# Neighbourhood attention on one core: one two-bank P V tile and one normalization for both jobs of a pair, and a reordered first step

## The chip, the cores and the metric

The kernel runs on one core of a Trainium2 chip. Times are device microseconds (us). TensorE is called PE here (PEld is its weight load), VectorE DVE, ScalarE ACT, GpSimd POOL, SyncE SP. A profile shows one execution; a time given for a kernel is the median of its runs.

## The reference

The input is an image of 224 by 224 pixels with 192 channels. Every pixel attends to 49 neighbours: 7 rows by 7 columns with a distance of 2 between them, the window being moved inwards at the border.

```python
qkv = x @ wqkv                                  # C = 192
q, k, v = qkv[..., :C], qkv[..., C:2*C], qkv[..., 2*C:]
r0 = clip(ir - 6, 0, H - 1 - 12)                # 7 rows, 2 apart
c0 = clip(ic - 6, 0, W - 1 - 12)                # 7 columns, 2 apart
logits = einsum('bnc,bnkc->bnk', q, kn) * C ** -0.5
p = softmax(logits)
out = einsum('bnk,bnkc->bnc', p, vn) @ wo
```

## The kernel before

**Tiling.** As neighbours are 2 apart, the image falls into even and odd rows (`rc`) and even and odd columns (`cc`). A step is 16 rows of one row class: 14 steps, `steps` in line 573, row classes taking turns. A step has 14 slots `s` of 8 columns in each column class; a slot is a job, and jobs 2m and 2m+1 are pair m of the step. So there are 7 pairs in a step and 98 in all, numbered k.

**Operands.** The weights are multiplied together at the start (`AW` from Wq and Wk, `WP` from Wv and Wo). x is loaded transposed in 14 bands of 16 rows (`load_items`, line 145: three transposing DMAs on SP, of which the one with k = 1 fills `X1`, tile names xa and x). From a band, POOL copies (DVE for the first ones) make `XB` (`xb_items`, line 158) and the sorted strips `XS` (`sort_items`, line 167). Out of these PE makes, for a coming step, G (`g_items`, line 405: `whole` and `halves`, the latter through a tile gx that two POOL copies spread, line 460) and V (`v_item`, line 347: 8 matmuls into one bank, copied to `VF`). `VD` is V shifted by half a slot; it is filled by DMAs `vd_low` and `vd_high` (lines 354 and 358), in step 0 for the next step also by `first_vd`.

**A pair.** `stage1` makes the scores of both jobs in two PSUM banks and their maxima (nmx, DVE, line 503); `stage1b` the exponentials p (ACT, line 511). `stage2` transposes p on PE into one bank and copies it to pt_sb (DVE, line 523; ACT in most of the last step). `stage3` is P V: 16 matmuls for a pair, 8 for each job, into a bank o_ps for each job; columns 192 and 193 of it hold the sums of p. `stage4a` takes their reciprocals (rs, line 538), `stage4` multiplies (line 552; for the last three pairs the second job on ACT, line 550) into an SBUF tile o_sb and issues the output DMAs.

**Outputs.** A slot other than 0 is written by one DMA of 16 rows on SP (line 558), or, in the first and the last step where the 16 rows fall into two runs, by two, some of them on POOL. Slot 0 holds the border columns of both sides: 10 small DMAs (15 in the first and in the last step) go into a list `pool_q` and are issued by POOL (line 571), at most four entries of the list in a pass; copies for coming steps are put ahead of them. The slot's tile (o_s0) is read until the last of them has landed. Its pool has two buffers, that of the other slots (o_sb) six.

**Order.** The loop (line 629) is written out by hand and every engine keeps the order in which its instructions were issued (`in_order`). Pass k issues: scores of pair k; p of its first job; P V of pair k-2 and the normalization of its first job; G halves (`w64`); p of the second job; the transposes of pair k-1 and their copy; the normalization of the second job of pair k-2; then DMAs, one of the three loads of a coming band (`ld.pop`, line 679: passes 0, 1 and 2 of a step), and the G and V of the next step (`w128`). In step 0 the first two passes carry the 14 V items of step 0 itself as well.

**PSUM.** Eight banks: two for the scores, one for transposed p, two of pool `ps_o` for o_ps, three of pool `ps_g` that G, V and others take in turn. A buffer of a pool goes to the next tile when one is free, not in a fixed turn: the V tiles of the built program stand in banks 6, 5, 7, 6, 5, 7, 6, 7, 6, 6, 5, 7 and so on.

Of the kernel before, what the change touches and what calls it, by code (L numbers as in the profile page):

```python
# [21 lines left out]
NSLOT = 14  # L22
# [6 lines left out]
C = 192  # L29
# [37 lines left out]
def _win(t, p0, pn, off, dims):  # L67
    a = t[:]
    ps = a.ap[0][0]
    return bass.AP(a.tensor, a.offset + p0 * ps + off, [[ps, pn]] + [list(d) for d in dims])  # L70
# [28 lines left out]
def kernel(  # L99
# [15 lines left out]
    pers = ctx.enter_context(tc.tile_pool(name="pers", bufs=1))  # L115
    ps_s = ctx.enter_context(tc.tile_pool(name="ps_s", bufs=1, space=PSUM))
    ps_t = ctx.enter_context(tc.tile_pool(name="ps_t", bufs=1, space=PSUM))
    ps_o = ctx.enter_context(tc.tile_pool(name="ps_o", bufs=2, space=PSUM))
    ps_g = ctx.enter_context(tc.tile_pool(name="ps_g", bufs=3, space=PSUM))
    x1_p = ctx.enter_context(tc.tile_pool(name="x1", bufs=2))  # L120

# [182 lines left out]
            nc.gpsimd.memset(_win(t, 0, 128, 112 * rc, [[128, 8], [1, 16]]), 0.0)  # L304
    wT_lo = setup.tile([128, 3, C], BF, name="wT_lo")
    wT_hi = setup.tile([64, 3, C], BF, name="wT_hi")
    n_t = 0
    for X in range(3):
        for (dt_, d0, dn) in ((wT_lo, 0, 128), (wT_hi, 128, 64)):
            tp = (ps_o, ps_g)[n_t % 2].tile([128, 1024], BF, name="tp_w", tag=("o", "pg")[n_t % 2])  # L310
            n_t += 1
            nc.tensor.transpose(tp[0:dn, 0:128], w_lo[:, X * C + d0: X * C + d0 + dn], ident[:])
            nc.tensor.transpose(tp[0:dn, 128:192], w_hi[:, X * C + d0: X * C + d0 + dn], ident[0:64, 0:64])
            nc.scalar.copy(out=dt_[:, X, :], in_=tp[0:dn, 0:192])
# [25 lines left out]
    def v_mms(pv, at):  # L340
        for cc in range(2):
            for pas in range(2):
                for h in range(2):
                    k = 1 if pas else 2 * cc
                    nc.tensor.matmul(pv[64 * h:64 * h + 64, cc * C:(cc + 1) * C], lhsT=at(k, h), rhs=WP[(cc, pas)][:], start=(pas == 0), stop=(pas == 1))  # L345

    def v_item(rc, cb):
        def emit(dve):
            pv = ps_g.tile([128, 512], F32, name="pv", tag="pg")
            v_mms(pv, lambda k, h: XS[rc][:, k, cb, 64 * h:64 * h + 64])  # L350
            evac(_win(VF[rc], 0, 128, cb * VP, [[193, 2], [1, C]]), pv[:, 0:2 * C].rearrange("p (t c) -> p t c", c=C), dve)
        return emit
# [52 lines left out]
    def g_items(rc, ti, s0, ns):  # L405
        rows = row_runs(rc, ti)
        w = 8 * ns

        def mm(pg, cc, p0, c0):

            out_ = []
            for (d0, dn, mem, pair) in col_runs(cc, 8 * s0, 8 * s0 + w):
                for (j, n, par, r) in rows:
                    o = _win(pg, p0, 64, j * w + d0, [[w, n], [1, dn]])
                    for pas in range(2):
                        X = (XA, XB)[pas][mem]
                        out_.append((o, AW[(mem, pas)][:, c0:c0 + 64], _win(X, 0, 128, _x(par, r, pair), [[RW, n], [1, dn]]), pas))
            return out_

        def both(a, b):  # L420
            for q in range(max(len(a), len(b))):
                for l_ in (a, b):
                    if q < len(l_):
                        (o, l, r, pas) = l_[q]
                        nc.tensor.matmul(o, lhsT=l, rhs=r, start=(pas == 0), stop=(pas == 1))  # L425

        def put(dst, off, pg, dve, p0=0, pn=128):

# [12 lines left out]
        def whole(cc):  # L441
            def emit(dve):
                pg = ps_g.tile([128, 512], F32, name="pg", tag="pg")
                both(mm(pg, cc, 0, OUT_A[cc]), mm(pg, cc, 64, OUT_A[cc] + 64))
                put(G[rc][cc], s0 * 128, pg, dve)
            return emit

        def halves(dve, direct=False):
            pg = ps_g.tile([128, 512], F32, name="pgh", tag="pg")
            pg1 = ps_o.tile([128, 512], F32, name="pgh", tag="o") if direct else pg  # L450
            both(mm(pg, 0, XDAT[0], OUT_B[0]), mm(pg1, 1, XDAT[1], OUT_B[1]))
            if direct:
                put(G[rc][0], (NSLOT + s0) * 128, pg, False, XDAT[0], 64)
                put(G[rc][1], (NSLOT + s0) * 128, pg1, True, XDAT[1], 64)
                return
            gx = work.tile([128, 512], BF, name="gx", tag="gx", bufs=3)
            put(gx, 0, pg, dve)
            for cc in range(2):
                p = XDAT[cc]
                nc.gpsimd.tensor_copy(out=G[rc][cc][p:p + 64, 1, s0:s0 + ns, :], in_=gx[p:p + 64, 0:ns * 128].rearrange("p (s q) -> p s q", q=128))  # L460

        return [whole(0), whole(1), halves]
# [59 lines left out]
        J.pt = work.tile([128, 8, 128], BF, name="pt_sb", tag="pt_sb")  # L522
        (nc.scalar.copy if J.n == NSTEP - 1 and J.m < 5 else nc.vector.tensor_copy)(out=J.pt[:], in_=pt_ps[:])  # L523

    def stage3(J, ab):
        rc, s = J.rc, 2 * J.m + ab
        o_ps = (ps_o if J.k < NP - 1 else ps_g).tile([128, 512], F32, name="o_ps", tag="o" if J.k < NP - 1 else "pg")
        V = (VD[rc], VF[rc])
        for cc in range(2):
            for q in range(2):  # L530
                for h in range(2):
                    nc.tensor.matmul(o_ps[64 * h:64 * h + 64, cc * 193:cc * 193 + 193], lhsT=J.pt[:, 4 * ab + 2 * cc + q, 64 * h:64 * h + 64],  # L532
                                     rhs=V[h][:, (s - 1 + q) % NSLOT, cc * C:cc * C + 193], start=(q == 0), stop=(q == 1))
        J.o_ps[ab] = o_ps

    def stage4a(J, ab):
        J.rs[ab] = stat.tile([128, 2], F32, name="rs", tag="rs")
        nc.vector.reciprocal(out=J.rs[ab][:], in_=J.o_ps[ab][:, C:C + 2])
        return J.rs[ab]

    def stage4(J, ab):
        rc, ti, s, o_ps = J.rc, J.ti, 2 * J.m + ab, J.o_ps[ab]
        rs = J.rs.get(ab) or stage4a(J, ab)
        if s > 0:
            o_sb = work.tile([128, 2, C], BF, name="o_sb", tag="o_sb", bufs=6)
        else:
            o_sb = work.tile([128, 2, C], BF, name="o_s0", tag="o_s0")
        if J.k >= NP - 3 and ab == 1:
            for cc in range(2):
                nc.scalar.mul(o_sb[:, cc, :], o_ps[:, 194 * cc:194 * cc + C], rs[:, cc:cc + 1])  # L550
        else:
            nc.vector.tensor_tensor(out=o_sb[:], in0=_win(o_ps, 0, 128, 0, [[194, 2], [1, C]]),  # L552
                                    in1=rs[:].unsqueeze(2).to_broadcast([128, 2, C]), op=ALU.mult)
        prow = _rows(rc, ti)
        if s > 0:
            for (j0, nj, r0, rstep) in _aff_runs(prow):
# [18 lines left out]
    for n, (ti, rc) in enumerate(steps):  # L575
        for m in range(7):
            J = Pair()
            J.n, J.ti, J.rc, J.m, J.k, J.o_ps, J.s, J.rs = n, ti, rc, m, len(pairs), {}, {}, {}
            pairs.append(J)
    NP = len(pairs)  # L580

# [47 lines left out]
    for k in range(NP + 2):  # L629
# [20 lines left out]
        if k == NP:  # L650
            stage2(pairs[k - 1])
        if k >= 2:
            stage3(pairs[k - 2], 0)
            stage3(pairs[k - 2], 1)
            if k >= NP:
                stage4a(pairs[k - 2], 0)
                stage4a(pairs[k - 2], 1)
            stage4(pairs[k - 2], 0)
            if k == NP - 1:
                stage4a(pairs[k - 2], 1)  # L660
        for it in w64:
            it(False)
        if J:
# [1 line left out]
        if 1 <= k < NP:  # L665
            stage2(pairs[k - 1])
        if k >= 2:
            stage4(pairs[k - 2], 1)
        if not J:
            continue  # L670

        if m == 1 and 0 < n and n + 1 < NSTEP:
            vd_low(rc1, 9 if n == 1 else 7, 14)
        if n == 0 and m in (4, 6):
            vd_low(0, *((0, 5) if m == 4 else (5, 9)), nc.scalar)
        if 0 < n and m == 5 and n + 2 < NSTEP:
            vd_low(J.rc, 0, 7)
        if ld:
            ld.pop(0)()
        for i, it in enumerate(w128):  # L680
            it(n == 0 and i % (2 if m < 3 else 3) == 1)
            if n == 0 and it is v0[6]:
                vd_high(0, 13, 14)
                vd_high(0, 0, 6)
            if n == 0 and it is v0[13]:
                vd_high(0, 6, 13)
            if it is vs[6]:
                vd_high(rc1, 0, 7)
            if it is vs[13]:
                vd_high(rc1, 7, 14)  # L690
# [67 lines left out]
```

## Time and profile before

| | us |
|---|---|
| median of 3 runs (lowest, highest) | 364.18 (363.53, 366.75) |
| the profiled execution | 362.85 |
| its span, first to last instruction | 361.1 |
| PE busy in the span | 335.6 |
| DVE, ACT, POOL busy | 313.7, 307.5, 285.6 |
| first pair's scores start | 19.6 |
| first slot of steps 0, 1, 2, 3 normalized | 36.5, 67.1, 91.7, 114.3 |

In the profile an engine is busy while an instruction runs on it; a wait is put down to the instruction that ended last before it. A group has its line, engine, operation, the tiles written and read, and a count. The matmuls' ends are modelled. The last row of the table tells where the steps lie: later ones follow every 21.8 to 23.5 us, step 0 takes 30.5 and step 1 24.6 us.

### The profile page before, as it was taken

How to read it: one execution, taken by the hardware profiler on the slowest of the kernel's cores; microseconds unless marked ns; L12 is line 12 of the kernel's file. 1: busy time of each engine (PE TensorE's matmuls, PEld its weight loads, DVE VectorE, ACT ScalarE, POOL GpSimd, SP SyncE). 2: the span in 40 equal slices, each digit the busy share in tenths (PEclk: the TensorE clock that was granted, in tenths of full speed). 3: DMA queues.
4: the chain of work that ended last, by engine and by line, in shares of the span. 5: the costliest groups of instructions: out<-in, count | busy, mean ns of one | idle time of the engine just before them, and what ended most of it. 6: DMA issues, size and time to landing. Idle time of an engine off the chain costs nothing.

```text
span 361.1 us, 19455 instructions
## 1 busy us (share of the span) xinstructions
PE 335.6 (93%) x8104; PEld 305.8 (85%) x8104; DVE 313.7 (87%) x743; ACT 307.5 (85%) x821; POOL 285.6 (79%) x456
## 2 busy tenths in 40 slices
PE   3988888998999999999999999999999999999881
PEld 1676777997999899999989999899999999999671
DVE  8967987887998998989989999898998889989992
ACT  3654767997998999989999999999989989999792
POOL 8976799999896986959969699696995878374094
PEclk9999999999999999999999999999999999999998
DMA  9999986697988979899799998988989965634432
GB/s 188 204 175 180 174 172 148 146 199 162 202 177 201 196 164 190 186 194 192 168 183 181 197 190 177 161 213 180 198 178 192 191 146 121 143 97 108 103 80 77
DMA packets 137778, 60.79 MB, mean 168 GB/s; under 512 B 88841, under 2 KB 137166, under 8 KB 137691
## 3 DMA queue, kind: packets, MB, share of 16 engines
q1 hardware_dynamic: 130133, 56.37, 78.3%
q0 software_dynamic: 5520, 1.73, 2.7%
q10 hardware_dynamic: 2038, 1.47, 2.2%
q8 instruction: 63, 1.03, 1.2%
q14 instruction: 24, 0.20, 0.2%
HBM read 0.29 MB, written 19.27 MB: 54 GB/s over the span
## 4 chain that ended last, share of the span: by engine, by line
PE 69%; POOL 10%; DVE 8%; ACT 6%; DMA 3%; issue 2%; SPq 1%; POOLq 0%; DVEq 0%; ACTq 0%
PE pv L345 16%; PE s L501 15%; PE o_ps L532 14%; PE pg L425 10%; PE pt_ps L521 9%; PE pgh L425 5%; POOL out_dram L571 4%; ACT p L511 3%; DVE xb L160 2%; POOL xs L170 2%; POOL out_dram L558 2%; DMA out_dram<-o_sb 1%; DMA vd<-vf 1%; ACT vf L335 1%; DVE nmx L503 1%
## 5 line engine op out<-in xcount | busy, mean ns | idle before, releaser
L511 ACT ACTIVATE p<-s,nmx 128x224 bf16<-128x224 f32 x392 | 149.8, 450 | 24.5 <-DVE nmx L503 22.8
L503 DVE TENSOR_REDUCE nmx<-s 128x2 f32<-128x392 f32 (+1 forms) x196 | 102.4, 564 | 19.9 <-PE s L501 19.4
L552 DVE TENSOR_TENSOR o_sb<-o_ps,rs 128x384 bf16<-128x384 f32 x179 | 99.8, 557 | 7.1 <-DMA out_dram<-o_sb 0.9
L460 POOL COPY g<-gx 64x512 bf16<-64x512 bf16 (+1 forms) x110 | 61.8, 562 | 52.9 <-ACT gx L335 47.1
L345 PE MATMUL pv<-wp,xs 128*64 128x192 bf16 x1624 | 92.7, 250 | 7.1 <-POOL xs L170 1.9
L345 PEld LDWEIGHTS <-xs 128*64 128x64 bf16 x1624 | 78.5, 111 | 20.5 <-issue 8.8
L335 ACT CAST vf<-pv 128x384 bf16<-128x384 f32 x193 | 87.6, 518 | 9.6 <-PE pv L345 5.2
L571 POOL DMA_DIRECT2D out_dram<-o_s x150 | 84.2, 568 | 1.1 <-issue 1.1
L532 PE MATMUL o_ps<-vd,pt_sb 128*64 128x193 bf16 x784 | 82.2, 246 | 2.9 <-ACT pt_sb L523 2.1
L501 PE MATMUL s<-xa,g 128*64 128x196 bf16 (+7 forms) x990 | 82.2, 233 | 1.6 <-issue 0.5
L532 PE MATMUL o_ps<-vf,pt_sb 128*64 128x193 bf16 x784 | 82.1, 246 | 0.0
L501 PE MATMUL s<-xb,g 128*64 128x196 bf16 (+7 forms) x990 | 81.8, 232 | 0.3 <-ACT g L335 0.3
L501 PEld LDWEIGHTS <-g 128*64 128x64 bf16 x1980 | 77.6, 110 | 3.6 <-issue 2.5
L532 PEld LDWEIGHTS <-pt_sb 128*64 128x64 bf16 x1568 | 71.3, 109 | 4.9 <-ACT pt_sb L523 3.2
L523 DVE COPY pt_sb<-pt_ps 128x1024 bf16<-128x1024 bf16 x93 | 63.7, 686 | 5.4 <-PE pt_ps L521 0.6
L521 PE MATMUL pt_ps<-ident,p 128*64 128x128 bf16 x1568 | 63.9, 219 | 0.0
L521 PEld LDWEIGHTS <-p 128*64 128x64 bf16 x1568 | 57.0, 110 | 5.2
L335 ACT CAST g<-pg 128x512 bf16<-128x512 f32 (+4 forms) x136 | 57.6, 471 | 2.0 <-PE pg L425 2.0
L425 PEld LDWEIGHTS <-aw 128*64 128x64 bf16 x1320 | 54.1, 110 | 4.1 <-issue 0.7
L425 PE MATMUL pg<-xb,aw 128*64 128x512 bf16 (+9 forms) x440 | 53.9, 269 | 0.6 <-DVE xb L160 0.6
L425 PE MATMUL pg<-xa,aw 128*64 128x512 bf16 (+9 forms) x440 | 52.0, 270 | 0.0
L170 POOL COPY xs<-xa 128x896 bf16<-128x896 bf16 x50 | 45.1, 928 | 1.4
(75 smaller groups left out, 282.8 us busy)
## 6 DMA issues: line engine op xcount, KB each, us to landing
vd<-vf SPq DMA_DIRECT2D x49, 336.9 KB
out_dram<-o_sb SPq DMA_DIRECT2D x156, 96.0 KB
out_dram<-o_sb SPq DMA_DIRECT2D x26, 78.0 KB
out_dram<-o_s POOLq DMA_DIRECT2D x78, 9.0 KB, 3.9
vd<-vf SPq DMA_DIRECT2D x2, 337.8 KB
vd<-vf ACTq DMA_DIRECT2D x2, 336.9 KB
xa<-in_x_dram SPq DMA_TRANSPOSE x28
out_dram<-o_s POOLq DMA_DIRECT2D x26, 15.0 KB, 3.1
```

The costliest lines, as they stand in the source:

```text
L335: nc.scalar.copy(out=out_, in_=in_)
L345: nc.tensor.matmul(pv[64 * h:64 * h + 64, cc * C:(cc + 1) * C], lhsT=at(k, h), rhs=WP[(cc, pas)][:], start=(pas == 0), stop=(pas == 1))
L425: nc.tensor.matmul(o, lhsT=l, rhs=r, start=(pas == 0), stop=(pas == 1))
L460: nc.gpsimd.tensor_copy(out=G[rc][cc][p:p + 64, 1, s0:s0 + ns, :], in_=gx[p:p + 64, 0:ns * 128].rearrange("p (s q) -> p s q", q=128))
L501: nc.tensor.matmul(o, lhsT=w, rhs=r, start=(pas == 0), stop=(pas == 1))
L503: nc.vector.tensor_reduce(out=nmx[:], in_=_win(s_ps, 0, 128, lo, [[256, 2], [16, 14], [1, 16 - lo]]), axis=AX.XY, op=ALU.max, negate=True)
L511: nc.scalar.activation(out=J.p[:, ab, cc, :, z:z + 112].rearrange("p q (r k) -> p q r k", k=8), in_=_win(s_ps, 0, 128, cc * 256, [[8, 2], ...
L521: nc.tensor.transpose(pt_ps[64 * h:64 * h + 64, 4 * ab + 2 * cc + q, :], J.p[:, ab, cc, q, 64 * h:64 * h + 64], ident[:])
L523: (nc.scalar.copy if J.n == NSTEP - 1 and J.m < 5 else nc.vector.tensor_copy)(out=J.pt[:], in_=pt_ps[:])
L532: nc.tensor.matmul(o_ps[64 * h:64 * h + 64, cc * 193:cc * 193 + 193], lhsT=J.pt[:, 4 * ab + 2 * cc + q, 64 * h:64 * h + 64], rhs=V[h][:, ( ...
L552: nc.vector.tensor_tensor(out=o_sb[:], in0=_win(o_ps, 0, 128, 0, [[194, 2], [1, C]]), in1=rs[:].unsqueeze(2).to_broadcast([128, 2, C]), op ...
L571: pool_q.append(lambda dst=dst, p=p, m=n * nj, cc=cc: nc.gpsimd.dma_start(out=dst.rearrange("j i c -> i j c"), in_=o_sb[p:p + m, cc, :]))
```

## The change

Both jobs of a pair get one tile of two banks (`ps_o` has now one buffer of that size), written by all 16 P V matmuls, then read by one reciprocal of 4 sums and one multiplication of 768 elements a partition into one o_sb tile for both jobs. Both stand ahead of the copy of transposed p; before, the second job's two stood behind it. The last three pairs keep the normalization in two parts. The o_sb tiles are now four of pair size; slot 0 has no tile of its own any more. Around the first step: the transposes of the weights use `ps_g` alone; in passes 0 and 1 the fourth and fifth V item take the two banks of `ps_o`; the two `vd_low` of step 0 are issued by SP instead of ACT; and the loads of step 0 are issued in passes 0, 2 and 4 instead of 0, 1 and 2.

```diff
-    ps_o = ctx.enter_context(tc.tile_pool(name="ps_o", bufs=2, space=PSUM))
+    ps_o = ctx.enter_context(tc.tile_pool(name="ps_o", bufs=1, space=PSUM))
...
-            tp = (ps_o, ps_g)[n_t % 2].tile([128, 1024], BF, name="tp_w", tag=("o", "pg")[n_t % 2])
-            n_t += 1
+            tp = ps_g.tile([128, 1024], BF, name="tp_w", tag="pg")
...
+    spare = []
+
     def v_item(rc, cb):
         def emit(dve):
-            pv = ps_g.tile([128, 512], F32, name="pv", tag="pg")
+            pv = spare.pop(0) if spare else ps_g.tile([128, 512], F32, name="pv", tag="pg")
...
-            pg1 = ps_o.tile([128, 512], F32, name="pgh", tag="o") if direct else pg
+            pg1 = ps_o.tile([128, 2, 512], F32, name="pgh", tag="o")[:, 0, :] if direct else pg
...
+    def stage3(J):
+        rc = J.rc
+        if J.k < NP - 1:
+            o = ps_o.tile([128, 2, 512], F32, name="o_ps", tag="o")
+            J.o_ps = [o[:, ab, :] for ab in range(2)]
+            J.o_2 = o
+        else:
+            J.o_ps = [ps_g.tile([128, 512], F32, name="o_ps", tag="pg") for ab in range(2)]
...
+    def stage4a(J, ab):
+        if J.rs is None:
+            J.rs = stat.tile([128, 2, 2], F32, name="rs", tag="rs")
+            J.o_sb = work.tile([128, 2, 2, C], BF, name="o_sb", tag="o_sb", bufs=4)
+        if ab is None:
+            nc.vector.reciprocal(out=J.rs[:], in_=_win(J.o_2, 0, 128, C, [[512, 2], [1, 2]]))
+        else:
+            nc.vector.reciprocal(out=J.rs[:, ab, :], in_=J.o_ps[ab][:, C:C + 2])
+
+    def stage4b(J, ab, eng):
+        if ab is None:
+            nc.vector.tensor_tensor(out=J.o_sb[:], in0=_win(J.o_2, 0, 128, 0, [[512, 2], [194, 2], [1, C]]),
+                                    in1=J.rs[:].unsqueeze(3).to_broadcast([128, 2, 2, C]), op=ALU.mult)
...
-            stage3(pairs[k - 2], 0)
-            stage3(pairs[k - 2], 1)
...
+            P = pairs[k - 2]
+            stage3(P)
+            if k < NP - 1:
+                stage4a(P, None)
+                stage4b(P, None, nc.vector)
+            else:
...
+            stage5(P, 0)
...
-            stage4(pairs[k - 2], 1)
+            if k >= NP - 1:
+                stage4b(P, 1, nc.scalar)
+            stage5(P, 1)
...
-            vd_low(0, *((0, 5) if m == 4 else (5, 9)), nc.scalar)
+            vd_low(0, *((0, 5) if m == 4 else (5, 9)))
...
-        if ld:
+        if ld and (n > 0 or m in (0, 2, 4)):
             ld.pop(0)()
+        if k < 2:
+            o = ps_o.tile([128, 2, 512], F32, name="pv", tag="o")
         for i, it in enumerate(w128):
+            if k < 2 and i in (3, 4):
+                spare.append(o[:, i - 3, :])
```

`stage5` holds the output DMAs as `stage4` had them.

More of the change, by code (lines that the diff above doesn't have):

```diff
@@ L306 @@
     wT_hi = setup.tile([64, 3, C], BF, name="wT_hi")
-    n_t = 0
     for X in range(3):
         for (dt_, d0, dn) in ((wT_lo, 0, 128), (wT_hi, 128, 64)):
-            tp = (ps_o, ps_g)[n_t % 2].tile([128, 1024], BF, name="tp_w", tag=("o", "pg")[n_t % 2])
-            n_t += 1
+            tp = ps_g.tile([128, 1024], BF, name="tp_w", tag="pg")
             nc.tensor.transpose(tp[0:dn, 0:128], w_lo[:, X * C + d0: X * C + d0 + dn], ident[:])
@@ L523, in stage2 @@
         (nc.scalar.copy if J.n == NSTEP - 1 and J.m < 5 else nc.vector.tensor_copy)(out=J.pt[:], in_=pt_ps[:])
-    def stage3(J, ab):
-        rc, s = J.rc, 2 * J.m + ab
-        o_ps = (ps_o if J.k < NP - 1 else ps_g).tile([128, 512], F32, name="o_ps", tag="o" if J.k < NP - 1 else "pg")
-        V = (VD[rc], VF[rc])
[L529 to L534, printed above, removed]
@@ L536, in stage4a @@
-    def stage4a(J, ab):
[L537 to L545, printed above, removed]
-        else:
-            o_sb = work.tile([128, 2, C], BF, name="o_s0", tag="o_s0")
-        if J.k >= NP - 3 and ab == 1:
+    def stage3(J):
[6 more added lines that the diff above has]
+            J.o_ps = [ps_g.tile([128, 512], F32, name="o_ps", tag="pg") for ab in range(2)]
+        V = (VD[rc], VF[rc])
+        for ab in range(2):
+            s = 2 * J.m + ab
+            for cc in range(2):
+                for q in range(2):
+                    for h in range(2):
+                        nc.tensor.matmul(J.o_ps[ab][64 * h:64 * h + 64, cc * 193:cc * 193 + 193], lhsT=J.pt[:, 4 * ab + 2 * cc + q, 64 * h:64 * h + 64],
+                                         rhs=V[h][:, (s - 1 + q) % NSLOT, cc * C:cc * C + 193], start=(q == 0), stop=(q == 1))
@@ new lines, in stage4a @@
+    def stage4a(J, ab):
+        if J.rs is None:
[3 more added lines that the diff above has]
+            nc.vector.reciprocal(out=J.rs[:], in_=_win(J.o_2, 0, 128, C, [[512, 2], [1, 2]]))
+        else:
+            nc.vector.reciprocal(out=J.rs[:, ab, :], in_=J.o_ps[ab][:, C:C + 2])
[3 more added lines that the diff above has]
+                                    in1=J.rs[:].unsqueeze(3).to_broadcast([128, 2, 2, C]), op=ALU.mult)
+        elif eng is nc.vector:
+            nc.vector.tensor_tensor(out=J.o_sb[:, ab], in0=_win(J.o_ps[ab], 0, 128, 0, [[194, 2], [1, C]]),
+                                    in1=J.rs[:, ab, :].unsqueeze(2).to_broadcast([128, 2, C]), op=ALU.mult)
+        else:
@@ L549, in stage4, with stage5 @@
             for cc in range(2):
[L550 to L553, printed above, removed]
+                nc.scalar.mul(J.o_sb[:, ab, cc, :], J.o_ps[ab][:, 194 * cc:194 * cc + C], J.rs[:, ab, cc:cc + 1])
+    def stage5(J, ab):
+        rc, ti, s, o_sb = J.rc, J.ti, 2 * J.m + ab, J.o_sb[:, ab]
@@ L577 @@
             J = Pair()
-            J.n, J.ti, J.rc, J.m, J.k, J.o_ps, J.s, J.rs = n, ti, rc, m, len(pairs), {}, {}, {}
+            J.n, J.ti, J.rc, J.m, J.k, J.s, J.rs = n, ti, rc, m, len(pairs), {}, None
             pairs.append(J)
@@ L652 @@
         if k >= 2:
-            stage3(pairs[k - 2], 0)
-            stage3(pairs[k - 2], 1)
[L655 to L660, printed above, removed]
+            P = pairs[k - 2]
[4 more added lines that the diff above has]
+            else:
+                stage4a(P, 0)
+                if k >= NP:
+                    stage4a(P, 1)
+                stage4b(P, 0, nc.vector)
+                if k == NP - 1:
+                    stage4a(P, 1)
+            stage5(P, 0)
         for it in w64:
```

## The prediction

> **What bounds the kernel now.** First the busy time by stage (us; PE, PEld, DVE, ACT, POOL, each with its count; clock, DMA share, GB/s).
>
> ```profile
> 17.00:50.00 33.00, 28.05 (x668) 23.72 (x666) 25.82 (x57) 20.42 (x57) 25.20 (x43) 1.00 1.11 183
> 50.00:64.00 14.00, 12.30 (x288) 10.50 (x286) 11.22 (x27) 10.38 (x29) 13.38 (x19) 1.00 0.68 152
> 64.00:97.00 33.00, 31.47 (x705) 28.26 (x703) 27.84 (x68) 29.14 (x79) 31.00 (x48) 1.00 0.83 171
> 97.00:325.00 228.00, 227.00 (x5766) 213.28 (x5763) 206.04 (x492) 213.16 (x577) 182.81 (x274) 1.00 0.88 177
> ```
>
> From 97 to 325 PE is busy for 227.0 of 228 us: an engine that gets lighter there gives back 1 us at the most. Idle PE lies in steps 0 and 1 (5.0 + 1.7 + 1.5 = 8.2 us from 17 to 97) and in the tail. Who ends those waits (us in total, times, longest), PE from 17 to 97:
>
> ```profile
> PE pv L345 <- POOL xs L170: 1.9, 3, 0.7
> PE pv L345 <- DVE g L333: 1.6, 2, 0.8
> PE pv L345 <- ACT g L335: 1.4, 4, 0.6
> ...
> PE o_ps L532 <- DMA vd<-vf: 0.5, 1, 0.5
> ```
>
> V waits for a bank to be copied out (DVE, ACT) or for its sorted strips (POOL). The POOL waits are the last ones, at 60.3 and 84 to 85.7 us, so the third view is POOL's instructions in order of time (start and duration in us):
>
> ```profile
> 52.59 0.58 POOL L558 DMA_DIRECT2D out_dram<-o_sb  x1
> 53.21 3.39 POOL L160 COPY xb<-x 64x1792 bf16<-64x1792 bf16 x2
> 56.66 1.80 POOL L170 COPY xs<-xa 128x896 bf16<-128x896 bf16 x2
> ```
>
> and the fourth the chain that ended last:
>
> ```profile
> 82.97 2.69 POOL xs L170 x3
> 85.66 0.04 issue
> 85.71 0.68 PE pv L345 x11
> ```
>
> POOL works from 43.14 to 85.65 without a pause over 0.13 us, and the V matmul of step 2 starts 0.06 us later. **So the end follows POOL's position in step 0, then PE.** When POOL copies band 3 (53.21) is the number to predict.
>
> **1. One normalization.** Per pair before: two reciprocals at 159 ns and two multiplications at 557, 1.43 us. The merged multiplication has no row; it costs no less than 557 (one of today's) and no more than 1114 (two). DVE's casts from f32 PSUM give a slope: 384 elements 560 ns, 512 elements 684, 0.97 ns an element, so 557 + 384 x 0.97 = 930; I take 0.95 us. With 0.16 for the reciprocal, 1.11: DVE gains 0.32 us a pair, 31 us in 95, behind a busy PE: nothing. [...]
>
> What moves is pt_sb, now behind the whole multiplication. A pass without G halves, DVE and then the weight load that reads pt_sb:
>
> ```profile
> 163.75 0.16 DVE L538 RECIPROCAL rs<-o_ps 128x2 f32<-128x2 f32 x1
> 163.94 0.56 DVE L552 TENSOR_TENSOR o_sb<-o_ps,rs 128x384 bf16<-128x384 f32 x1
> 164.42 0.68 DVE L523 COPY pt_sb<-pt_ps 128x1024 bf16<-128x1024 bf16 x1
> ```
>
> ```profile
> 165.63 0.11 PEld L532 LDWEIGHTS <-pt_sb 128*64 128x64 bf16 x1
> ```
>
> pt_sb ends at 165.10 and its reader starts at 165.63: 0.53 us. The longer multiplication takes 0.39 of it; 0.14 is left, so nothing. In passes with halves 0.75 is there. If the cover goes, each 0.1 us over costs 0.1 in three passes of some eleven steps, 3.3 us; at 1114 ns 0.02 is lacking, 0.7 us.
>
> The reciprocal now waits for both jobs. In the pass at 166 us the matmuls of the first job end at 166.29, of the second at 166.64, and the first job's reciprocal starts at 166.68 already today, behind the maxima (165.73 to 166.77). Cost nothing. The next P V waits for the whole tile: it is free by 164.9, needed at 165.63.
>
> **2. The o_sb ring.** Slot 0's 10 transfers go out late. Step 4: tile written at 137.07, last transfer issued 152.20, landed 156.64; pair 4 of the step normalizes at 149.65, pair 5 at 153.21, pair 6 at 156.95. The tile is now one of the ring's four. If a free buffer goes to who comes, as with the V banks, the others turn in three, the distance of the six halves today, and pair 1's outputs have landed at 147.9. A strict turn can't be: step 0's last slot-0 transfers stand in passes 7 and 8, behind POOL copies that need results DVE would only make after pass 6. Should pair 6 get the held tile, it waits 0.9, 1.4 and 0.9 us in steps 6 to 8, less some 0.5 of cover. Between 0 and 2 us; I take 0.4, nearest to the free buffer.
>
> **3. Two more banks for V in passes 0 and 1.** Banks then last for five V instead of three. Stepping the copies through (ACT 0.45 us apart, DVE 0.5), G is ready 0.9 us earlier after pass 0, 2.1 after pass 1. Then P V of pair 0 waits for VD, which lands at 34.55 whatever PE does (issued at 29.97): 1.7 goes back. Later V waits of pass 2 (0.74 us idle) vanish; POOL's gx copy moves from 37.31 to 36.1. POOL would then reach band 3 at 52.0: **-1.2**.
>
> **4. The third load of band 3** moves from pass 2 to pass 4. SP's order:
>
> ```profile
> 42.81 1.48 SPq L154 DMA_TRANSPOSE x<-in_x_dram  x1
> 44.38 2.61 SPq L558 DMA_DIRECT2D out_dram<-o_sb  x3
> 47.04 1.14 SPq L242 DMA_DIRECT2D xb<-xb  x1
> 48.29 2.58 SPq L558 DMA_DIRECT2D out_dram<-o_sb  x3
> ```
>
> The load was issued at 42.81 and the semaphore POOL waits for was full at 48.10, 5.3 us; three later ones took 5.4 to 6.05. In its new place SP has ahead of it: V's copies (31.4), vd_high 0.6, first_vd 2.7, G rows 3.1, G columns 1.2 (39.3 with gaps), then 1.0 + the second load 2.9 + 2.6 + 1.1 + 2.6 + the moved vd_low 0.7, in all 50.7. Pass 1 is rid of a load, so the long ones may fall to 0.6 each, the load to 1.9; then SP waits for o_sb (40.6, 44.2) and the start is 47.5. Landing: 52.8 to 56.8. I take 54.2, nearer to the early end, as less is in flight there (DMA share 0.68 against 1.11). POOL stands for 2.2 us where it had no wait; xb, xs, gx copies, outputs and all of step 1 queue behind it. **+1.0 against 53.21** (-1.2 to +3.6). The moved vd_low saves ACT nothing: at 45.53 it lay beside a running copy. The weights' transposes in three banks end behind 0.6 us of cover: PE waits for DVE until 18.52.
>
> **5. Tail.** Slot 1's output leads POOL's last row of DMAs; it starts when the second job is normalized (342.44). Merged, that is 342.15: **-0.3**.
>
> **Sum**: the profiled execution has 361.1 of span and 362.85 in all; +1.0 + 0.4 - 0.3 = +1.1 gives 363.95. The median of the runs stands 1.33 above it: **365.3**.
>
> **Rivals.**
> - Faster: the load lands by 52.0, giving -1.2 - 0.3: 362.7, still within 1%. More only if POOL isn't the bound and PE's waits on copies (3.7 us) and on the strips go as well, 5 us: 359. For: DVE and ACT get lighter. Against: POOL's unbroken row. Chance 0.08 each.
> - Slower, the ring: the held tile goes to the pair that comes next. Deciding point: which of two tiles is freed first in the built order. At pair 6 of steps 6 to 8 and the last pair of step 1 (tile landed at 90.54, wanted at 88.06) DVE stands for 5.7 us, PE for some 4 more: 369. One pair earlier, at pair 5, the waits in steps 2 to 10 are 2.0 to 4.2, 28 us in sum, 23 past the cover: 387. For: POOL is late with these transfers in every step. Against: in program order pairs 1 to 3 are written out first. 0.14 and 0.06.
> - The load lands at 56.8: 367.9. For: SP is back to back from 23 to 56 us. 0.08.
> - The wait for both jobs: where DVE stands ready at the first job's end, the normalization starts up to 0.35 us later, pt_sb lacks 0.35 - 0.14 = 0.21 in three passes of eleven steps: 7 us, 372. Against: in the pass at 166 us the maxima end behind both. 0.03. [...]
> - The merged operation merges nothing (1114 ns): 366. 0.04.
>
> **Numbers.** The forecast, as told, has 0.49. Within 1% (360.5 to 367.8, about what a measurement of this kernel can tell from no change): 0.49 + 0.08 + 0.04 + half of the late load 0.04 = 0.65; slower 0.14 + 0.06 + 0.03 + 0.04 = 0.27; faster 0.08. The range reaches from just under the mild faster case to just over the mild ring case, 361.9 to 369.8, and leaves 0.08 + 0.06 + 0.03 = 0.17 out.
>
> **What would show it.** One reciprocal and one multiplication a pair of 0.93 to 0.96 us ahead of pt_sb; V waits in passes 0 and 1 gone; POOL idle before the first xb copy by some 2 us, ended by the load of x; the first V of step 2 near 86.7; from there PE unbroken. I am wrong if POOL has no such wait, or if DVE shows waits of o_sb for the slot-0 transfers in several steps.

## The result, and the profile after

The changed kernel takes 368.95 us (median of 6 runs, 368.13 to 370.47) against 363.86 of the kernel before (6 runs, 362.62 to 366.75): a ratio of 1.0157, 95% interval 1.0129 to 1.0184. By the medians it is slower by 5.1 us, by the ratio, which is used from here on, by 5.7, where 365.3, no difference that can be told, was forecast; the time lies within the range given, 361.9 to 369.8. The profiled execution took 370.47 in all and 368.7 from first to last instruction. It is the longest of its six, as that of before was below its median, so the two traces lie 7.6 us apart, and not all of this is the change. One profiled execution among the experiments (the DVE copies of band 3 in the kernel with the merged normalization, 366.49) stands 4 us above its kernel's median; only its waits up to 97 us are read.

The table by stage, as before (us; PE, PEld, DVE, ACT, POOL, each with its count; clock, DMA share, GB/s):

```profile
17.00:50.00 33.00, 26.43 (x634) 22.52 (x635) 24.91 (x51) 19.25 (x54) 24.54 (x42) 1.00 0.86 159
50.00:64.00 14.00, 10.03 (x221) 8.07 (x217) 9.47 (x18) 9.02 (x24) 9.90 (x14) 0.96 0.71 142
64.00:97.00 33.00, 32.09 (x690) 30.78 (x692) 24.55 (x45) 27.59 (x74) 31.03 (x52) 0.91 0.82 177
97.00:325.00 228.00, 224.18 (x5655) 209.51 (x5652) 186.13 (x346) 210.22 (x570) 181.03 (x267) 1.00 0.90 176
```

DVE is lighter by 19.9 us between 97 and 325 (206.04 before), as meant. PE is idle for 4.0 us between 50 and 64 (1.7 before) and for 6.6 between 17 and 50 (5.0), and from 64 to 97 it is busy at a granted clock of 0.91: busy, but slow. From 97 on it lacks 3.8 us of 228 (1.0 before). PE's waits from 17 to 97 (total, times, longest):

```profile
PE pv L343 <- POOL xs L170: 3.3, 1, 3.3
PE pv L343 <- DVE vf L331: 2.3, 4, 0.7
...
PE pgh L425 <- POOL xb L160: 1.1, 1, 1.1
```

The waits for POOL's strips were three of 0.7 us at most; now there is one of 3.3, with a wait of 1.1 for POOL's copy of band 3 ahead of it. POOL's own row around band 3 (start, duration, and in brackets the idle time before and what ended it):

```profile
56.84 3.39 POOL L160 COPY xb<-x 64x1792 bf16<-64x1792 bf16 x2 [3.53 <-DMA x<-in_x_dram]
60.29 1.80 POOL L170 COPY xs<-xa 128x896 bf16<-128x896 bf16 x2
```

POOL is ready at 53.31, where it was at 53.21 before, and stands for 3.53 us until x has landed. SP's queue shows why it is late; the moved shift of V is right ahead of the load:

```profile
47.53 2.54 SPq L571 DMA_DIRECT2D out_dram<-o_sb  x3
50.17 1.24 SPq L356 DMA_DIRECT2D vd<-vf  x1
51.51 1.92 SPq L154 DMA_TRANSPOSE x<-in_x_dram  x1
```

The chain that ended last, where it leaves POOL for PE:

```profile
60.29 1.80 POOL xs L170 x2
...
63.89 0.94 POOL xs L170
...
64.88 1.33 PE pv L343 x9
```

From there PE doesn't wait again up to 97: it has lost so much that POOL is ahead of it. Set against each other by the first maxima of the same pair (DVE's nmx), the changed kernel is 0.3 us ahead at the start of step 1 (58.23 against 58.55), 5.7 behind at the pair after next, 3.6 behind at the start of step 3, 7.3 at step 11 and 7.0 at the last pair. So there are three pieces: +3.6 in steps 0 to 2, some +3.6 in steps 4 to 10, and the tail. For the second piece, PE's waits from 97 to 325 in the changed kernel ("issue" is a stop in which PE waits for nothing that the profile shows):

```profile
PE s L501 <- issue: 1.8, 2, 1.2
PE pv L343 <- ACT g L333: 1.5, 2, 1.1
PE o_ps L539 <- issue: 0.2, 1, 0.2
```

In the kernel before these are 0.5 us of stops and 0.2 for ACT, so they make up 2.9 of the 3.6.

### The profile page after: what moved, and what is told of

Same layout as the page of the kernel before. It is cut to its first block, busy times and chain, and to the rows that moved or that the text cites. A ratio compares the mean times of both kernels' runs of the same rounds, so it can differ in the third digit from the quotient of the medians.

```text
span 368.7 us, 19126 instructions
## 1 busy us (share of the span) xinstructions
PE 337.3 (91%) x8104; PEld 308.1 (84%) x8104; DVE 291.6 (79%) x553; ACT 307.8 (83%) x821; POOL 285.1 (77%) x456
## 4 chain that ended last, share of the span: by engine, by line
PE 67%; POOL 11%; DVE 8%; issue 4%; ACT 4%; DMA 4%; POOLq 0%; SPq 0%; DVEq 0%; ACTq 0%
PE pv L343 15%; PE s L501 14%; PE o_ps L539 14%; PE pg L425 10%; PE pt_ps L521 9%; PE pgh L425 5%; POOL out_dram L584 3%; POOL xs L170 3%; ACT p L511 3%; DMA out_dram<-o_sb 2%; POOL xb L160 2%; POOL g L460 2%; DVE xb L160 2%; POOL out_dram L571 1%; DMA vd<-vf 1%
## 5 line engine op out<-in xcount | busy, mean ns | idle before, releaser
L343 PE MATMUL pv<-wp,xs 128*64 128x192 bf16 x1624 | 91.7, 250 | 9.9 <-POOL xs L170 3.3
L555 DVE TENSOR_TENSOR o_sb<-o_ps,rs 128x768 bf16<-128x768 f32 x95 | 91.0, 958 | 10.4 <-DMA out_dram<-o_sb 6.1
L501 PE MATMUL s<-xa,g 128*64 128x196 bf16 (+8 forms) x990 | 83.3, 234 | 2.5 <-issue 1.8
L584 POOL DMA_DIRECT2D out_dram<-o_sb x150 | 84.2, 568 | 1.1 <-issue 1.1
L501 PE MATMUL s<-xb,g 128*64 128x196 bf16 (+8 forms) x990 | 82.8, 233 | 0.3 <-ACT g L333 0.3
L501 PEld LDWEIGHTS <-g 128*64 128x64 bf16 x1980 | 78.5, 111 | 4.8 <-issue 3.5
L521 PE MATMUL pt_ps<-ident,p 128*64 128x128 bf16 x1568 | 64.7, 220 | 0.0
L521 PEld LDWEIGHTS <-p 128*64 128x64 bf16 x1568 | 57.9, 110 | 4.9
L425 PEld LDWEIGHTS <-aw 128*64 128x64 bf16 x1320 | 54.2, 111 | 7.1 <-issue 3.3
```

Of the source, the lines that this page charges most:

```text
L501: nc.tensor.matmul(o, lhsT=w, rhs=r, start=(pas == 0), stop=(pas == 1))
L521: nc.tensor.transpose(pt_ps[64 * h:64 * h + 64, 4 * ab + 2 * cc + q, :], J.p[:, ab, cc, q, 64 * h:64 * h + 64], ident[:])
L555: nc.vector.tensor_tensor(out=J.o_sb[:], in0=_win(J.o_2, 0, 128, 0, [[512, 2], [194, 2], [1, C]]), in1=J.rs[:].unsqueeze(3).to_broadcast([ ...
L584: pool_q.append(lambda dst=dst, p=p, m=n * nj, cc=cc: nc.gpsimd.dma_start(out=dst.rearrange("j i c -> i j c"), in_=o_sb[p:p + m, cc, :]))
```

## The experiments

The first theory was that two of the prediction's rivals had come true side by side, the late load and the ring of tiles, and that the two add up. The changed kernel's DVE has the ring's waits (total, times, longest, 17 to 340 us):

```profile
DVE o_sb L555 <- DMA out_dram<-o_sb: 6.1, 8, 1.2
```

Seven of these eight stand in steps 3 to 10, six of them at pair 6, which was taken to have been given slot 0's tile; the eighth stands at pair 2 of step 1.

**The load back in pass 2**

```diff
-        if ld and (n > 0 or m in (0, 2, 4)):
+        if ld:
```

> The changed kernel with one edit undone: band 3's third load goes back to pass 2. Theory (the late load and the ring both cost, and add up): POOL's 3.53 us wait for x is gone, PE's 1.1 and 3.3 us waits at 59 to 65 us shrink to the 0.7 us of before and TensorE's granted clock stays at 1.00 there; the ring's waits stay (DVE 5 to 7 us, PE 1.5 to 2). Time 365.5 (364.8 to 366.3). Rival (the load is the whole loss): 363.9. Rival (the load is a side show, since POOL's lateness was there before too): 368 or more.

Measured: 370.29 us, ratio 1.0154 (1.0099 to 1.0209). No gain at all. POOL's wait is gone, as expected, and the second pair of step 1 stands at +0.1 us, but then DVE stops at pair 1 of step 1 (its row in this kernel):

```profile
75.77 0.96 DVE L555 TENSOR_TENSOR o_sb<-o_ps,rs 128x768 bf16<-128x768 f32 x1 [4.60 <-DMA out_dram<-o_sb]
```

That pair has the tile that step 0's slot 0 was written into. Its 15 transfers are issued by POOL until 72.0 us, and the last lands at 75.45. PE waits 4.2 us behind it (o_ps for pt_sb). In the changed kernel the same transfers land at 79.28, and the pair with that tile (pair 2 of step 1) waits only 0.58 us, since the late load has made DVE late as well. The two losses don't add up: **the late load covers the ring.**

**Slot 0 in a tile of its own**

```diff
-            J.o_sb = work.tile([128, 2, 2, C], BF, name="o_sb", tag="o_sb", bufs=4)
+            J.o_sb = work.tile([128, 2, 2, C], BF, name="o_sb", tag="o_sb" if J.m else "o_s0", bufs=3 if J.m else 1)
```

> The changed kernel with pair 0's output tile out of the ring: a tile of its own for each step's first pair, three tiles in turn for the others (the same memory as four). Theory: DVE's waits for out_dram (8 times, 6.1 us) go to zero, PE gets back the 1.5 to 2 us that they cost it from 97 us on, POOL's wait for x stays at 3.5: time 367.2 (366.4 to 367.9). Rival (DVE's waits lie beside a busy PE and cost nothing): 368.9. Rival (the ring is the larger of the two losses, as in the prediction's mild case): 365.0.

Measured: 378.36 us, 1.0392 (1.0347 to 1.0436). The edit gave slot 0 a single buffer; before the change it had two, and so the first pair of step 1 now waits for the transfers of step 0 (DVE's row):

```profile
79.47 0.96 DVE L555 TENSOR_TENSOR o_sb<-o_ps,rs 128x768 bf16<-128x768 f32 x1 [7.84 <-DMA out_dram<-o_sb]
```

From step 3 on the kernel has no wait for a tile any more, and it loses 0.7 us up to the last pair (+11.3 to +12.0) where the changed kernel loses 3.3. It looked as if the ring cost 2.6 us there; the kernel with two single tiles, below, speaks against this: it has no ring with slot 0 either and loses 2.7 (+2.4 to +5.1).

**Both, and both without the spare banks and with vd_low on ACT**

```diff
-            pv = spare.pop(0) if spare else ps_g.tile([128, 512], F32, name="pv", tag="pg")
+            pv = ps_g.tile([128, 512], F32, name="pv", tag="pg")
...
-            vd_low(0, *((0, 5) if m == 4 else (5, 9)))
+            vd_low(0, *((0, 5) if m == 4 else (5, 9)), nc.scalar)
```

> Both edits: the load in pass 2 and a tile of its own for pair 0. Left of the change: one normalization a pair, the spare banks for V, vd_low on SP. Theory (two losses that add up, and nothing else in the change costs): 363.9 (363.2 to 364.6). Rival (the wait of one reciprocal for both jobs, or one P V tile for two, costs too): 366 or more, with PE waits on pt_sb or o_ps in every step from 97 us on. Rival (the lighter DVE pays once the two are gone): 362 or less.

> As the run with both edits, and V's spare banks and the moved vd_low undone too: only the merged normalization, its two-bank tile and the weights' transposes in three banks are left. Theory (the spare banks bring nothing, since two V in one tile wait for each other's copy: pass 1 started 0.71 us later in the changed kernel): 0.5 us under the run with both edits, 363.4. Rival (the prediction's step 3, spare banks bring 1.2 us): 1.2 us over it, 365.1. Merged normalization by itself: nothing, 363.4 to 364.2 against 363.9 of before.

Measured: 373.67 (1.0270, 1.0219 to 1.0322) and 370.93 (1.0192, 1.0155 to 1.0230). Both have the same stop of 8.9 and 7.8 us at the first pair of step 1, so neither tells what the merged normalization costs in step 1. From step 3 to the last pair the first goes from +8.3 to +8.6 and the second from +6.2 to +6.0: with no wait for tiles, one normalization for both jobs costs nothing there.

**Two single tiles for slot 0.** The new theory (a wait that covers another) asks for an edit that brings back the two buffers in the same memory: slot 0's pair takes two multiplications, the first into one of two single tiles, and the ring has three pair tiles.

```diff
-            J.o_sb = work.tile([128, 2, 2, C], BF, name="o_sb", tag="o_sb", bufs=4)
+            J.o_sb = work.tile([128, 2, 2, C], BF, name="o_sb", tag="o_sb", bufs=3)
+            J.o_s0 = work.tile([128, 2, C], BF, name="o_s0", tag="o_s0")[:] if J.m == 0 else J.o_sb[:, 0]
...
-        if ab is None:
+        if ab is None and J.m == 0:
+            stage4b(J, 0, eng)
+            stage4b(J, 1, eng)
+        elif ab is None:
```

> The changed kernel, with slot 0's output in two single tiles of its own as before the change (its pair takes two multiplications; the other six pairs of a step keep the merged one and turn in three tiles). New theory: step 0's slot-0 transfers stand last in POOL's list (issued until 75.5 us, landed 79.3); whichever pair of step 1 gets that tile stands still until then, and the late load, where it is kept, hides this wait, because everything before it is late as well. So here, with the load still late: no DVE wait for out_dram at all, POOL's wait of 3.5 us and PE's 4.4 us at 59 to 65 us stay, +3.6 us at the start of step 3 as in the changed kernel, nothing more up to the end: 367.3 (366.5 to 368.2). Rival (the late load is harmless once the ring is mended): 364. Rival (the merged normalization costs in itself): 369 or more.

> As the run before, and band 3's third load back in pass 2. Theory: both waits are gone, no stall of 4 to 9 us in step 1; pairs 8 and 9 at +0.1 against the kernel before, step 3 at 0 to +0.3, the end at 0: 364.0 (363.3 to 365.0). Rival (the merged normalization or the one P V tile costs in itself): 366 or more. Rival (a lighter DVE brings something now): 362.5 or less.

> As the run before, without V's spare banks and with vd_low on ACT's queue: the merged normalization of six pairs in seven alone. Theory: 363.7 (363.0 to 364.6), that is 0 to 0.7 us under the run before, since pass 2 begins 0.9 us earlier without the spare banks and POOL's band 3 at 52.7 instead of 53.3. Rival (the prediction's step 3): 1.2 us over it.

Measured, with each run taking one more part of the change away: 369.10 (1.0155, 1.0120 to 1.0191) with the load still late; 367.61 (1.0110, 1.0077 to 1.0144) with the load in pass 2; 364.99 (1.0023, 0.9995 to 1.0050) without the spare banks and with vd_low on ACT. The first stands 1.8 us above what was expected; it says that, with the load late, the ring costs nothing that can be measured: 1.0155 against 1.0157. (It is not free of waits for tiles, as was expected: DVE has two, 1.9 us, at pairs 3 and 4 of step 1.) The last, in which six pairs of seven have the merged normalization, says the same of that. The second missed: 367.6 where 364.0 was expected, which is where the rival stood by which the merged normalization costs in itself. But it is 2.6 us above the third, so a part that I had at 0 to 0.7 us, the spare banks or vd_low, costs several.

**The spare banks alone put back**

```diff
-            pv = ps_g.tile([128, 512], F32, name="pv", tag="pg")
+            pv = spare.pop(0) if spare else ps_g.tile([128, 512], F32, name="pv", tag="pg")
```

> The merged normalization alone (365.0 in its own runs) with V's two spare banks put back; vd_low stays on ACT's queue, the load in pass 2, slot 0 in tiles of its own. It splits the 2.6 us between that kernel and the one that had vd_low on SP's queue as well (367.6). Theory: the spare banks make pass 2 begin 0.95 us later and half of it is still there at step 1, 0.5 us; the rest is vd_low on SP, ahead of outputs and loads that step 1 waits for: 365.5 (364.8 to 366.2). Rival (the spare banks are all of it): 367.6. Rival (the prediction's step 3, they bring 1.2): 363.8.

Measured: 364.53, 1.0016 (0.9992 to 1.0040). The spare banks cost and bring nothing that can be measured; the difference to the kernel at 367.6 (3.4 us by the ratios) is vd_low on SP's queue, the one edit between the two. DVE's waits from 60 to 97 us in the two, with vd_low on SP and then on ACT:

```profile
DVE o_sb L559 <- DMA out_dram<-o_sb: 2.5, 2, 1.4
```

```profile
DVE o_sb L559 <- DMA out_dram<-o_sb: 0.4, 1, 0.4
```

SP has hardly a pause there (0.10 us between the rows of the changed kernel's queue above), and each vd_low takes 0.65 to 1.24 us of it. With it in SP's queue outputs of step 1 are issued later (the first after it at 62.31 against 61.70, a later one at 77.43 against 74.60), and pairs 3 and 4 wait for their tiles. At step 3 this is worth 0.4 us (+0.64 against +0.21). Up to the last pair the two traces part by another 1.9 us. There PE has 1.25 us of stops with no wait shown against 0.19, and 1.65 us of waits for ACT's copies of G against 1.05; the longest of these, 1.08 us at 273.94, follows a V shift that ACT had waited 1.68 us for. Why the queue of step 0 should set any of these is open: the two kernels are written the same from step 1 on. So the time that vd_low costs is measured, and all but 0.4 us of its cause is not shown.

**vd_low on SP in the kernel before**

```diff
-            vd_low(0, *((0, 5) if m == 4 else (5, 9)), nc.scalar)
+            vd_low(0, *((0, 5) if m == 4 else (5, 9)))
```

> The kernel before with one edit alone: V's two low shifts of step 0 (passes 4 and 6) go out on SP's queue instead of ACT's. Theory (SP is back to back there, so each of the two puts 0.7 us into its queue, and outputs and loads of step 1 land that much later, as in the pair of kernels at 367.6 and 364.5 that differ in this alone): 366 to 367. Rival (it costs only together with the pair tiles in turn of three, where a tile is free when the later of two outputs has landed; with single tiles there is room): 364, no change. Rival (ACT is relieved of 1.3 us of issuing, which pays): 363 or less.

Measured: 365.49, 1.0032 (1.0004 to 1.0060), between theory and rival. ACT does gain: the first pair of step 1 comes 1.1 us earlier than before (57.45 against 58.55). Then POOL's strips (1.6 us, PE's longest wait for them) and a DVE wait of 1.34 us for an output take that back. So the move costs 1.2 us (0.1 to 2.2) with single tiles, and some 3 with pair tiles. That it is more because a pair tile is free only when the later of its two outputs has landed is an argument that the runs don't show.

**The late load in the kernel before**

```diff
-        if ld:
+        if ld and (n > 0 or m in (0, 2, 4)):
```

> The kernel before with one edit alone: the loads of step 0 in passes 0, 2 and 4. vd_low is on ACT's queue as before, so SP reaches the third load about 1.2 us earlier than in the changed kernel, 50.3, and it lands at 55.6: POOL waits some 2.4 us at 53.2. Theory: +1.5 to +2.5 us, 366.0. Rival (it costs nothing, POOL's lead elsewhere takes it): 364. Rival (PE's pause makes the granted clock fall as in the changed kernel, 0.50 for some 6 us): 367.5.

Measured: 366.41, 1.0077 (1.0051 to 1.0104), +2.8 us. SP's and POOL's rows in this kernel:

```profile
50.42 1.47 SPq L154 DMA_TRANSPOSE x<-in_x_dram  x1
```

```profile
54.67 3.39 POOL L160 COPY xb<-x 64x1792 bf16<-64x1792 bf16 x2 [1.49 <-DMA x<-in_x_dram]
```

Issued at 50.42, in at 54.67: POOL waits for 1.49 us, and in this execution pair 1 of step 1 is 1.47 us late, one for one. The execution as a whole took 366.24, close to the median, and its granted clock does not fall before the end. It is 3.4 us behind the trace of before at the last pair; the 1.9 us beyond the stop come in steps 3 to 12, where PE has 1.71 us of stops with no wait shown (0.45 before) and waits 1.19 us for ACT's copies of G (0.20 before). So half of the price is the load's wait; how the rest hangs on the load is open. In other runs of this kernel the clock has a part too; see below.

**Band 3's copies on DVE.** If the change frees DVE, it may pay to give DVE something to do. The two copies into xb are moved behind the G copies of passes 5 and 6, in the kernel with the merged normalization (slot 0 in its own tiles) and in the kernel before:

```diff
             it(n == 0 and i % (2 if m < 3 else 3) == 1)
+            if n == 0 and m in (5, 6) and i == 1:
+                xb_items(3, dve)[m - 5]()
...
-            add = {0: sort_items(1, 1, pool), 1: sort_items(2, 1, pool), 3: sort_items(2, 0, pool), 5: xb_items(3, pool) + sort_items(3, 0, pool)}.get(m, [])
+            add = {0: sort_items(1, 1, pool), 1: sort_items(2, 1, pool), 3: sort_items(2, 0, pool), 5: sort_items(3, 0, pool)}.get(m, [])
```

> The merged normalization alone, and the two copies of band 3 into xb (3.39 us on POOL at 52.7) given to DVE, behind its G copies of passes 5 and 6, where it waits 0.7 and 1.1 us for PE. Theory (the change only pays if what it frees on DVE takes work off POOL): POOL starts the strips of band 3 3.4 us earlier, PE's waits of 0.9 us at 60.7 and 1.2 us at 84 to 85 for them go: 363.0 (362.2 to 364.0). Rival (the copies, some 1.9 us in two passes, push DVE's maxima back and PE waits for those): 365 or more.

> The kernel before, with the same two copies on DVE and nothing else. If the room on DVE comes from the merged normalization, this gains less: PE's waits for DVE's G copies (0.8 us at 47.8 and at 57.5) grow by some 0.5 each while the waits for POOL (1.9 us) go: 363.2 (362.4 to 364.2) against 363.9. Rival (the room was there before, since DVE waits for PE in step 0): 362 or less, under the run with the merged normalization.

Measured: 362.44 (0.9948, 0.9916 to 0.9980) and 363.47 (0.9980, 0.9951 to 1.0009). The first is the one version that beats both kernels, by 1.9 us (0.7 to 3.1) against the kernel before and, by the ratios, by 7.6 against the changed one. The second can't be told from no change; neither can the two from each other, so that the merged normalization is what makes the room isn't shown. PE's waits from 57 to 97 us in the merged kernel, with the copies on POOL and then on DVE:

```profile
PE pv L343 <- POOL xs L170: 2.1, 3, 0.9
```

```profile
PE o_ps L539 <- DVE pt_sb L523: 1.9, 1, 1.9
PE pv L343 <- ACT g L333: 1.1, 1, 1.1
```

The waits for POOL are gone, and a wait for a tile is next (DVE 2.3 us at pair 3 of step 1): here too one wait stands behind another.

## Why the prediction was right or wrong

**The kernels as a ladder** from before to after (ratio times 363.9, less that of the step below):

| part added | ratio | us |
|---|---|---|
| merged normalization, slot 0 in its own tiles (and the weights' transposes in three banks) | 1.0023 | +0.8 |
| spare banks for V | 1.0016 | -0.3 |
| vd_low on SP | 1.0110 | +3.4 |
| third load in pass 4 | 1.0155 | +1.6 |
| slot 0 in the ring | 1.0157 | +0.1 |

Each ratio has an interval of 0.9 to 1.3 us to either side, and a difference of two more than that. So vd_low is the one part of the ladder that stands clear of noise; the first two and the last are nothing that can be told, and the load's +1.6 may be anything from 0 to 3.4. The price of a part also hangs on its place on the ladder: alone in the kernel before, the load is +2.8, clear of noise, and vd_low +1.2, only just. The ring's +1.6 where the load is early (1.0154 against 1.0110) is not.

That the time came out within the range is luck in part: the upper end stood for the ring at 369, and the ring is not what costs. The prediction had no term for vd_low's place in the queue, for the clock and for PE's stops.

- **Step 1, one normalization: right.** The merged multiplication takes 958 ns (0.95 forecast) and the reciprocal 0.17 us; DVE is 22.1 us less busy in all (31 forecast), and it is worth nothing in the loop. DVE's rows in a pass of the changed kernel without halves:

```profile
170.89 0.17 DVE L548 RECIPROCAL rs<-o_ps 128x4 f32<-128x4 f32 x1
171.09 0.96 DVE L555 TENSOR_TENSOR o_sb<-o_ps,rs 128x768 bf16<-128x768 f32 x1
171.97 0.68 DVE L523 COPY pt_sb<-pt_ps 128x1024 bf16<-128x1024 bf16 x1
```

  The room between the end of pt_sb and the first weight load of it, worked out from the trace's rows, is 0.12 to 0.17 us in the passes 3 and 5 of steps 2 to 12 (0.14 forecast). In pass 1 there is more, but for four passes in which DVE had waited for a tile first: there the weight load follows pt_sb after 0.05 us, as it does behind the stop of 4.2 us in the kernel with the load back in pass 2, so PE does wait. The rivals "merges nothing" and "waits for both jobs" are out.
- **Step 2, the ring: right in size, wrong in place.** The waits stand at pair 6, where the step would have them if that pair gets the held tile, and they go with slot 0's tile out of the ring. DVE waits 6.1 us in all, and PE's weight loads stand idle in the four passes named above for 0.26, 0.30, 0.15 and 0.01 us, 0.7 in sum (0.4 forecast). The prediction called waits of o_sb in several steps a sign that it is wrong; they came, in six steps, and cost little. What the step left out is step 0, whose last transfer lands at 76.79 in the kernel before: one pair of step 1 is given that tile. In the traces this stops PE for 4.2 us with the load early and is covered with the load late.
- **Step 3, the spare banks: failed.** POOL came to band 3 at 53.31, no lead in place of 1.2. The fourth and fifth V item (numbers 3 and 4 of the list) have a bank each, but in one tile, and the fifth waits for the copy of the fourth. The changed kernel's V matmuls on PE from item 4 on, and DVE's copy of item 3:

```profile
24.71 1.18 PE L343 MATMUL pv<-wp,xs 128*64 128x192 bf16 x24 [0.65 <-DVE vf L331]
```

```profile
24.10 0.56 DVE L331 CAST vf<-pv 128x384 bf16<-128x384 f32 x1 [0.94 <-PE pv L343]
```

  The group at 24.71 starts with item 4 and was held until item 3's copy ended at 24.66. PE's waits for V's copies on DVE, which were to go, grew from 0.7 to 2.3 us up to 97 us. Pass 1 began 0.71 us later, pass 2 0.95 us. The time doesn't show it: 1.0016 with the spare banks, 1.0023 without.
- **Step 4, the load: right in mechanism, wrong in size.** The start was put at 47.5 to 50.7 and was 51.51. The main reason is step 3: the sum has SP past V's copies at 31.4, and SP's next V shift started at 33.74, since the lead did not come. The second load was shorter than counted (1.49 for 2.9) and vd_low longer (1.24 for 0.7). The landing was put at 54.2 within 52.8 to 56.8, and was 56.84, just past the far end. The term was +1.0; POOL's copy of band 3 is 3.6 us later than before, and the trace has +3.6 at step 3. In between, at pair 2 of step 1, it has +5.7: some 2 us of that are the clock (last section), and the waits that PE had there before and has no longer (1.5 us idle from 64 to 97 before) take most of them back. That vd_low was moved past nothing dear was the worse slip: the outputs and loads of step 1 behind it in the queue had no term. It is the largest step of the ladder, though the traces show the cause of 0.4 us only.
- **Step 5, the tail: wrong sign.** POOL's last row now has a pause that the merged multiplication ends, and the tail is 0.6 us longer from the last pair on, not 0.3 shorter. It is 0.63 or 0.64 us longer in all ten traces with the merged normalization and within 0.03 us of before in the three others without it. This is the one cost of the merged normalization that the traces show:

```profile
354.61 1.15 POOL L571 DMA_DIRECT2D out_dram<-o_sb  x2 [0.36 <-DVE o_sb L555]
```

- **First V of step 2 at 86.7, then PE unbroken**: POOL's wait came as told, ended by the load of x, but 3.5 us and not 2; and PE was no longer behind POOL by then. The chances of 0.08 for the late load and 0.27 for slower look low now: three costs without a term or with too small a one (the load, vd_low, the clock) lay on the same side, and the two gains set against them (the lead, the tail) did not come.

## What to carry to other kernels

An edit to a queue that is back to back cost 1.2 us here with single tiles and some 3 with pair tiles, for two issues of 0.65 to 1.24 us each: count what stands behind it, and who waits for those landings. Two waits in the same stretch can cover each other (the wait for slot 0's tile was 4.60 us with the load early and 0.58 with it late), so taking one away proves nothing of the other's price; undo them in all orders, or measure each alone in the kernel before. Merging small instructions on an engine that isn't the bound was worth nothing here (1.0023, 0.9995 to 1.0050), and cost 0.6 us in the tail, where that engine is waited for; filling the room with work from the engine that is the bound paid (0.9948, 0.9916 to 0.9980), but it isn't shown that the room came from the merge. And two banks in one tile were not two tiles here: the second group of matmuls started at 24.71, behind the end of the first one's copy at 24.66.

## What the runs showed of the hardware

**The clock fell behind a short pause, and not always.** In the changed kernel PE stands from 61.55 to 64.88 us, 3.33 us. The granted clock is 0.50 from 62.81 to 69.64, so PE runs at half the clock for 4.8 us after the pause (granted clock third from the right):

```profile
63.00:66.00 3.00, 1.12 (x15) 1.12 (x17) 0.00 (x0) 0.40 (x1) 2.96 (x6) 0.50 0.69 157
66.00:69.00 3.00, 3.00 (x43) 3.00 (x41) 1.23 (x3) 1.88 (x6) 2.90 (x6) 0.50 0.77 165
```

In the profiled execution of the kernel with two single tiles for slot 0 and the late load a pause of the same 3.33 us (60.50 to 63.83) left the clock alone:

```profile
63.00:66.00 3.00, 2.17 (x54) 2.18 (x56) 0.92 (x2) 1.15 (x3) 2.94 (x6) 1.00 0.94 209
```

At pair 2 of step 1 the first stands at +5.7 us and the second at +2.6. Of the 3.1 between them 1.05 is the load, in at 56.84 and at 55.79; the other 2 us go with the clock. Over the traces, a pause of 2.15 us (the late load in the kernel before) and this one of 3.33 left it alone; it fell with pauses of 3.32 (slot 0 in a tile of its own, and again there with one of 7.0), 3.33 (the changed kernel), 4.20 (the load back in pass 2), 6.9 (both edits, without the spare banks and with vd_low on ACT) and 8.01 us (both edits). The lowest mean clock of a stretch of 3 us behind these was 0.71 with the pause of 3.32, 0.50 or 0.51 with the others. Ahead of the two that fell at 3.3 us PE had stood for another 0.8 and 1.1 us, 1.3 us earlier, and ahead of the one that didn't it had not; whether that decides is open. In the kernel before with the late load alone the mean clock goes with the time from run to run: the four of ten runs at a mean clock of 0.988 or 0.989 took 367.5 to 368.4 us, the six at 0.991 to 0.997 took 364.2 to 366.6. How long PE's pauses were in those four isn't known, as the traced one is of the six. So, but for that one of 3.33 us, PE's pauses of 3.32 us and more in these traces had two prices, their length and the clock behind them. The late-load rival was priced with the first alone.

**PE's stops end behind a block of instructions.** In 12 of the 14 traces PE stops once or more, in all but one case between 154 and 190 us, with nothing to wait for. PE's row behind the longest stop in the changed kernel:

```profile
184.14 0.24 PE L501 MATMUL s<-xa,g 128*64 128x196 bf16 x1 [1.19 <-issue]
```

The DMA records show a block of 16 KB on a queue of instructions, from 181.80 to 182.75, and PE goes on 1.39 us after its end. The other three stops of the two traces end 1.39, 1.43 and 1.47 us after such a block (in the changed kernel at 164.02, in the kernel before at 155.61, in the changed one at 159.35), and the 24 stops of all the traces 1.24 to 1.69 us after one; so the queue is taken for PE's. That PE stands for want of instructions there is a reading of these times and not shown. Blocks come every 5 us or so; these four came 5.3 to 7.3 us after the one before, but for one. Gaps as long come some 20 times between 97 and 335 us in each of the two traces, mostly without a stop, so a late block alone doesn't make one; in the changed kernel 3 of the 63 blocks of that queue have a stop behind them. The stops sum to 0.5 us in the trace of before and 2.0 in that of after, which is 1.6 of the 7.6 us between the two traces. Whether the change makes them more frequent isn't settled: the kernels of the experiments have between 0 and 2.6 us of them.
